# A new written order for the opening of a windowed-attention and two-MLP kernel

## The chip, the core and the metric

The kernel runs on one core of one Trainium2 chip. The metric is device time in microseconds (us) of one execution. The engines are TensorE (PE; its weight loads are listed as PEld), VectorE (DVE), ScalarE (ACT), GpSimd (POOL) and SyncE (SP), which here only issues transfers (DMA). Each engine works through its own instructions in order and waits on semaphores for the others.

## The reference

Three stages follow each other. Attention, with 4 batches, 8 heads, 512 local and 32 global tokens and a head size of 64; its result, 2176 tokens by 512, is `x`. A gated MLP with hidden size 1536, and a second MLP with hidden size 2048 and a rational function.

```python
s_g = scale * q_g @ concat(k_g, k_l).T          # global queries see all keys
out_g = softmax(s_g) @ concat(v_g, v_l)
s_ll = where(abs(i - j) <= 32, scale * q_l @ k_l.T, -1e9)
s_l = concat(scale * q_l @ k_g.T, s_ll)         # local ones see a window and the 32 globals
out_l = softmax(s_l) @ concat(v_g, v_l)
x = concat(out_g, out_l)                        # -> (2176, 512)
g = x @ w_gate                                  # 512 -> 1536
x = (g * sigmoid(g) * (x @ w_val)) @ w_out      # 1536 -> 512
h = x @ w_in                                    # 512 -> 2048
P = a0 + a1*h + a2*h**2 + a3*h**3
Q = 1 + abs(b0)*abs(h) + abs(b1)*h**2
out = (P / (Q + 1e-6)) @ moe2_w_out             # 2048 -> 512
```

The weights come as 64-bit floats.

## The kernel before, in words

**Attention** is cut into 24 units. A local unit is a block of 128 queries of one batch with all 8 heads, in two halves p of 4 heads each; a batch has 4 of them. A global unit is the 32 global queries of one batch with 4 heads; each batch has 2, and they come 4 units behind their batch's first. Units 6 and 7 are the first global ones. A unit passes through `a_score` (L247, products of queries and keys into PSUM), `a_soft` (L294: for each head a least value with the mask on DVE, L304, and an exponential with its sum on ACT, L310), `a_trans` (L335: eight PE transposes, L341, the sums' reciprocals on DVE, two copies out of PSUM, L353 or L355), `a_pv` (L362: products with the values, L374, and the division on DVE, L380) and `a_out` (L403: four PE transposes, L410, and a copy into `x32`, the token matrix, on DVE, L412).

**The first MLP** runs in two passes. Pass a, which matters here, takes the first 4 of 12 hidden blocks f (NA = 4) over 8 token chunks of 256 or 288 columns. For each chunk c and each f there are a gate product, a value product and an outward product of 12 matmuls each (`mlp`, `hidden`, `outward`). Every operand is split into a high and a low part, and each product takes three matmuls (L490 to L492). In between, `hidden` has a tanh on ACT (L518), two products on DVE (L519, L526) and the split of the result (L123 on ACT, L126 on DVE). The token chunk itself is split by `split_xy`. Outward products add up in four PSUM tiles for a chunk, and `evac_a` copies them out after its last f.

**Weights** are fetched in tiles of 512 KB (`fetch`, L131) and turned into 32-bit floats in `to_f32`: a scaling on POOL (L141), a rounding on ACT (L143), and two instructions on DVE that join the halves (L144, L146). `first_finish` then splits the first 12 tiles, which are the three tiles of each of the four f, into a high part (ACT, L123) and a low part (POOL, L126). The later 24 tiles of the first MLP are converted in the background by the loader `bg` (L634) and stored to DRAM (`w1s`, L632); it has two stage buffers and keeps one tile ahead, and a tile's fetch is issued on SP behind the store of the tile before it.

**Order.** PE and SP run in program order (`tc.manual_schedule`). The other engines' order is set by a planner. `prologue` (L583) runs units 0 and 1 (all steps), a score of unit 2, two weight tiles and the split of chunk 0. "d" words there and the table `fill` put matmuls on a tile of zeros ahead of waits, 23 of them after the first 11. Then come the pairs (c, f) in order, chunk by chunk. `inject_a` (L594) is called three times in each, ahead of the value product, ahead of the outward product and behind it; it steps the weight loaders and, by `attend` (L462), runs a part of one attention step: transposes of unit t-1; scores of unit t; values of unit t-1 and output of unit t-2. At the start of chunk 2, units 0 to 9 have their scores and units 0 to 8 their values, and 4 background tiles have been converted; 16 attention steps and 20 tiles are left for the twenty pairs of chunks 2 to 6. Chunk 7 has none.

Of the kernel before, what the change touches and what calls it, by code (L numbers as in the profile page):

```python
# [10 lines left out]
F32 = mybir.dt.float32  # L11
# [10 lines left out]
S = SL + SG  # L22
# [55 lines left out]
def tile_attn_moe_moe(  # L78
# [165 lines left out]
    st_s, st_e, st_t, st_r, st_x = {}, {}, {}, {}, {}  # L244
    ps_tag = ["a"]

    def a_score(u):  # L247
# [30 lines left out]
        a_soft(u)  # L278

    def a_score2(u):  # L280
        b, qb, ps_ = units[u]
        if qb == 4:
# [9 lines left out]
            a_soft(u)  # L292

    def a_soft(u):  # L294
        b, qb, ps_ = units[u]
        mn = att.tile([128, 8], F32, tag="mn", name="mn", bufs=3)
        sm = att.tile([128, 8], F32, tag="sm", name="sm", bufs=4)
        e = att.tile([128, 1024], F32, tag="e", name="e", bufs=2)
        if qb < 4:
            s = st_s.pop(u)  # L300
            for p in ps_:
                for hh in range(4):
                    i = 4 * p + hh
                    nc.vector.tensor_tensor_reduce(  # L304
                        out=e[:, 128 * i:128 * i + 128], in0=s[p][:, 128 * hh:128 * hh + 128], in1=msk[:, qb],
                        op0=ALU.add, op1=ALU.min, scale=-SCALE, scalar=3.0e38, accum_out=mn[:, i:i + 1],
                    )
                for i in range(4 * p, 4 * p + 4):
                    c = slice(128 * i, 128 * i + 128)
                    nc.scalar.activation(  # L310
                        e[:, c], e[:, c], AF.Exp, bias=mn[:, i:i + 1], scale=-1.0,
                        accum_out=sm[:, i:i + 1],
                    )
        else:
            s0, s1 = st_s.pop(u)
# [5 lines left out]
            )  # L321
            nc.scalar.activation(e[:, 0:384], s0[:, 0:384], AF.Exp, bias=mn[:, 2:3], scale=SCALE,
# [3 lines left out]
        st_e[u] = (e, sm)  # L326

    fill = {("t", 1): 2, ("p", 0): 2, ("p", 1): 2, ("x", 1): 3}

    def filled(o, key):  # L330
        for _ in range(fill.get(key, 0)):
            nc.tensor.matmul(o, zero[:, 0:128], zero, start=True, stop=True)
        return o

    def a_trans(u):  # L335
        b, qb, ps_ = units[u]
        e, sm = st_e.pop(u)
        t = [psum(ps_tag[0]) for p in ps_]
        filled(t[0], ("t", u))
        for i in range(4 * len(ps_)):  # L340
            nc.tensor.transpose(t[i // 4][:, 128 * (i % 4):128 * (i % 4) + 128], e[:, 128 * i:128 * i + 128], ident)  # L341
# [20 lines left out]
    def a_pv(u):  # L362
# [4 lines left out]
        if qb < 4:  # L367
# [17 lines left out]
            if n < len(local):  # L385
                load_v(local[n])
# [587 lines left out]
```

## Time and profile before

| | us |
|---|---|
| median of 3 runs | 948.02 (947.64 to 948.88) |
| span of the profiled execution | 944.1 |
| first gate product of chunk 0 starts | 22.73 |
| first gate product of chunk 2 starts | 97.12 |
| first gate product of chunk 7 starts | 247.95 |

The span reaches from the first to the last instruction of one profiled execution. A page of the profile gives the busy time of each engine, the chain of work that ended last, and groups of instructions by line. A busy PE is not a PE at its peak: matmuls are pipelined and overlap in the listing, so that the distance from one start to the next tells their cost, and an instruction that is listed as long can have waited inside. Of pass a, 8 x 4 pairs of chunk and hidden block, the first eight end at 97.12 us.

### The profile page before, as it was taken

To read this page: it belongs to the slowest core of one execution; us is meant where nothing else is said; L and a number is where in the kernel's file an instruction comes from. 1 tells how busy PE (TensorE), PEld (TensorE's weight loads), DVE (VectorE), ACT (ScalarE), POOL (GpSimd) and SP (SyncE) were. 2 spreads that over 40 slices of the span, in tenths; PEclk is the share of its full clock that TensorE was granted. 3 is DMA by queue.
4 is the path that set the end of the run, shared out by engine and by line. 5 is a ranking of instruction groups with operands and counts; after the bars stand their busy time and mean duration, and the time that the engine had idled before them with its cause. 6 is when DMAs were issued, how large, how long until landed. Compare 5 with 4: busy or idle time off the path is not lost.

```text
span 944.1 us, 20305 instructions
## 1 busy us (share of the span) xinstructions
PE 915.8 (97%) x7906; PEld 846.5 (90%) x7906; DVE 664.2 (70%) x1576; ACT 570.5 (60%) x1354; POOL 115.5 (12%) x129
## 2 busy tenths in 40 slices
PE   7789999999999999999999999999999999999997
PEld 4578878888899999999999999999999999999996
DVE  5697667766656466555432569988888888888886
ACT  5665746664344343332322368888778788788796
POOL 2440000010133244111000001000000000000032
PEclk9899999999999999999999999999999999999999
DMA  9937858853561234454522230000010010010010
GB/s 339 365 118 245 290 188 277 273 174 115 181 209 71 85 104 134 156 172 167 164 72 72 72 109 1 1 15 20 1 34 1 0 34 1 1 34 1 1 34 24
DMA packets 51169, 102.77 MB, mean 109 GB/s; under 512 B 6912, under 2 KB 25984, under 8 KB 51072
## 3 DMA queue, kind: packets, MB, share of 16 engines
q1 hardware_dynamic: 51072, 101.47, 32.5%
q8 instruction: 62, 1.02, 0.4%
q14 instruction: 35, 0.29, 0.1%
HBM read 81.01 MB, written 20.45 MB: 107 GB/s over the span
## 4 chain that ended last, share of the span: by engine, by line
PE 73%; DMA 12%; DVE 6%; ACT 3%; issue 2%; POOL 1%; SPq 1%; POOLq 0%; ACTq 0%; DVEq 0%
PE b L491 14%; PE b L490 14%; PE b L492 14%; DMA stage<-in_w_dram 10%; PE a L871 6%; PE a L872 6%; PE a L870 6%; PE a L490 4%; PE a L491 4%; PE a L492 4%; DVE stage L144 2%; DVE stage L146 2%; ACT e L310 1%; POOL stage L141 1%; DMA v<-in_vw_dram 1%
## 5 line engine op out<-in xcount | busy, mean ns | idle before, releaser
L490 PE MATMUL b<-xy,wb 128*128 128x312 f32 (+3 forms) x632 | 198.0, 313 | 0.0
L491 PE MATMUL b<-xy,wb 128*128 128x312 f32 (+3 forms) x632 | 198.0, 313 | 0.0
L492 PE MATMUL b<-xy,wb 128*128 128x312 f32 (+3 forms) x632 | 197.7, 313 | 0.0
L490 PE MATMUL b<-xy,wa 128*128 128x256 f32 (+2 forms) x400 | 125.4, 314 | 2.1 <-DVE mn L304 1.7
L491 PE MATMUL b<-xy,wa 128*128 128x256 f32 (+2 forms) x400 | 121.7, 304 | 1.2 <-DVE xy L126 1.1
L490 PEld LDWEIGHTS b<-xy,wb 128*128 128x128 f32 x632 | 118.8, 188 | 2.6
L492 PE MATMUL b<-xy,wa 128*128 128x256 f32 (+2 forms) x400 | 121.2, 303 | 0.0
L491 PEld LDWEIGHTS b<-xy,wb 128*128 128x128 f32 x632 | 118.8, 188 | 2.4
L492 PEld LDWEIGHTS b<-xy,wb 128*128 128x128 f32 x632 | 118.8, 188 | 0.0
L123 ACT CAST h<-s 128x312 fp32r<-128x312 f32 (+3 forms) x88 | 38.7, 440 | 128.7 <-DVE s L529 91.3
L820 ACT ACTIVATE t<-b,cst 128x384 f32<-128x384 f32 (+1 forms) x94 | 61.3, 652 | 56.6 <-PE b L492 53.9
L529 DVE TENSOR_TENSOR s<-s,b 128x312 f32<-128x312 f32 (+1 forms) x56 | 26.7, 476 | 94.3 <-PE b L492 89.5
L834 DVE TENSOR_TENSOR t<-t,b 128x384 f32<-128x384 f32 (+1 forms) x94 | 49.9, 531 | 44.3 <-ACT a L821 43.9
L141 POOL TENSOR_SCALAR stage<-stage 128x512 f32<-128x512 f32 x68 | 46.9, 693 | 273.7 <-DMA stage<-in_w_dram 242.7
L490 PEld LDWEIGHTS b<-xy,wa 128*128 128x128 f32 x400 | 76.3, 191 | 4.4 <-ACT e L310 1.9
L144 DVE SCALAR_TENSOR_TENSOR stage<-stage 128x512 int32<-128x512 int32 x68 | 48.6, 714 | 43.5 <-POOL stage L141 33.1
L491 PEld LDWEIGHTS b<-xy,wa 128*128 128x128 f32 x400 | 75.9, 190 | 3.3 <-DVE xy L126 2.1
L492 PEld LDWEIGHTS b<-xy,wa 128*128 128x128 f32 x400 | 75.7, 189 | 0.0
L126 DVE TENSOR_TENSOR h<-s,h 128x312 fp32r<-128x312 f32 (+3 forms) x88 | 44.1, 501 | 37.3 <-ACT h L123 37.3
L143 ACT ACTIVATE stage<-stage 128x512 int32<-128x512 uint32 x68 | 46.0, 681 | 39.2 <-DMA stage<-in_w_dram 28.0
L872 PE MATMUL a<-wb,g 128*128 128x512 f32 x170 | 66.8, 393 | 0.3 <-POOL g L844 0.3
L871 PE MATMUL a<-wb,g 128*128 128x512 f32 x170 | 67.1, 395 | 0.0
(160 smaller groups left out, 2261.8 us busy)
## 6 DMA issues: line engine op xcount, KB each, us to landing
stage<-in_w_dram SPq DMA_DIRECT2D x68, 512.0 KB, 4.3
v<-in_vw_dram SPq DMA_DIRECT2D x16, 512.0 KB, 6.6
v<-in_vw_dram SPq DMA_DIRECT2D x16, 384.0 KB, 5.5
w1s<-stage SPq DMA_DIRECT2D x24, 256.0 KB, 2.5
stage<-w1s SPq DMA_DIRECT2D x12, 512.0 KB, 6.1
w2s<-stage SPq DMA_DIRECT2D x20, 256.0 KB, 2.4
stage<-w2s SPq DMA_DIRECT2D x10, 512.0 KB, 3.7
out_dram<-x SPq DMA_DIRECT2D x17, 256.0 KB, 2.7
```

Source lines behind the costliest of these rows:

```text
L126: eng_lo.tensor_tensor(out=lo, in0=src, in1=hi.bitcast(F32), op=ALU.subtract)
L141: nc.gpsimd.tensor_scalar(out=high.bitcast(F32), in0=high.bitcast(F32), scalar1=2.0 ** -112, scalar2=1.0, op0=ALU.mult, op1=ALU.mult)
L143: nc.scalar.activation(low, low.bitcast(U32), AF.Copy, bias=0.25, scale=0.905 * 2.0 ** -29)
L144: nc.vector.scalar_tensor_tensor(out=low, in0=high, scalar=3, in1=low, op0=ALU.logical_shift_left, op1=ALU.bitwise_or)
L490: nc.tensor.matmul(o, w[:, 0, wsl], x[:, 0, xsl], start=first, stop=False)
L491: nc.tensor.matmul(o, w[:, 0, wsl], x[:, 1, xsl], start=False, stop=False)
L492: nc.tensor.matmul(o, w[:, 1, wsl], x[:, 0, xsl], start=False, stop=last)
L820: nc.scalar.activation(pt[n], h, AF.Identity, bias=NA2, scale=NA3)
L834: nc.vector.tensor_tensor(out=t, in0=t, in1=h, op=ALU.mult)
L870: nc.tensor.matmul(o, g[:, 0, gsl], w[:, 0], start=(f == 0), stop=False)
L871: nc.tensor.matmul(o, g[:, 0, gsl], w[:, 1], start=False, stop=False)
L872: nc.tensor.matmul(o, g[:, 1, gsl], w[:, 0], start=False, stop=(f == F2 - 1))
```

## The change

The first eight pairs, chunks 0 and 1, are laid out anew, with what lies before them.

- The steps of a unit become small functions (`a_least`, `a_exp`, `a_turn`, `a_copy`, `a_sums`, `a_value`, `a_norm`, `a_back`, `a_store`), as do those of a weight tile (`w_scale`, `w_round`, `w_join`, `w_high`, `w_low`), of a chunk split (`y_high`, `y_low`) and of a pair (`h_gate`, 3 of the 12 matmuls at a time, `h_tanh`, `h_times`, `h_high`, `h_low`).
- One string of words, `opening`, gives their order on every engine, also that of the transfers on SP ("@"), and for copies and low parts which of two engines has them ("*"). It covers units 0 to 7, the scores and exponentials of unit 8, the twelve first weight tiles, and chunks 0 and 1, both for f = 0, then both for f = 1, and so on. Units 0 to 3 stand ahead of the first outward product, units 0 and 1 ahead of the first gate product.
- Outward products of the two chunks share PSUM tiles, 256 columns each, which zero matmuls open; `evac_a` copies both.
- From chunk 2 on, the loop is that of before. Its twenty pairs up to chunk 7 hold 17 attention steps and 24 background tiles, two of them in each fifth pair.
- `bg` keeps three tiles ahead, over six stage buffers.
- Fillers in the opening: 3 and 5, and the first 11 stay.

The diff, cut:

```diff
+    def a_turn(u, p):
         b, qb, ps_ = units[u]
...
+        t = filled(psum(ps_tag[0]))
+        for i in range(4):
+            nc.tensor.transpose(t[:, 128 * i:128 * i + 128], e[:, 512 * p + 128 * i:512 * p + 128 * i + 128], ident)
...
-    U0 = 2
+    U0 = 9
...
+    step_at = dict(zip([n for n in range(8, 27) if n not in (12, 20)], range(U0, NU + 2)))
...
+    HALF = 256
+    seq_a = [(c, f) for f in range(NA) for c in range(2)] + [(c, f) for c in range(2, NCA) for f in range(NA)]
...
     def outward(key, f, w, first, last):
-        if first:
+        side = key == ("a", 1)
+        pair = key in (("a", 0), ("a", 1))
+        if first and not side:
             for j in range(KD):
                 accs[j] = psum("a")
+                if pair:
+                    nc.tensor.matmul(accs[j], zero[:, 0:128], zero, start=True, stop=False)
         h = hs.pop((key, f))
+        o = HALF * side
         for j in range(KD):
-            mm3(accs[j][:, :w], wt1[f, 2], slice(128 * j, 128 * j + 128), h, slice(0, w), first, last)
+            mm3(accs[j][:, o:o + w], wt1[f, 2], slice(128 * j, 128 * j + 128), h, slice(0, w),
+                first and not pair, last and (side or not pair))
...
-    prologue("s0 d4 s1 d5 t0 p0 t1 x0 p1 w x1 y s2", warm,
-             lambda: [split_xy(("a", 0), chunks_a[0], k) for k in range(KD)])
...
+    def h_gate(c, f, m, k):
+        key, w = ("a", c), HALF
+        if k == 0:
+            half[c, f, m] = filled(psum("b"))
+        mm3(half[c, f, m][:, :w], wt1[f, m], slice(128 * k, 128 * k + 128), xs[key, k], slice(0, w),
+            k == 0, k == KD - 1)
...
+    def w_round(i, eng):
+        lo = raw[i].rearrange("p (c t) -> p c t", t=2)[:, :, 0]
+        nc.scalar.activation(lo, lo.bitcast(U32), AF.Copy, bias=0.25, scale=0.905 * 2.0 ** -29)
...
+    opening = (
+        "@q0 @k0 @m0 @m1 @w0 @k1 @q1 @q2 @v00 @w1 S0 @k2 @m2 @v01 A0 F0 M00 @q3 M01 E00 @v10 S1 D0 @v11 "
+        "E01 T00 @K1 M11 C00* E11 d3 T01 R0 M10 P00 H0 C01* T11 E10 L0* @v20 F1 A1 R1 d5 T10 @q4 C11 D1 "
+        "@K0 S2 C10 @w2 H1 P01 M21 @w3 L1 S3 N0 E21 @v21 M20 P10 X0 M31 @v30 E20 P11 T21 Z0 N1 E31 @v31 "
+        "T20 R2 M30 X1 @q5 C20* Z1* T31 @w4 C21 y03* y01* C31 Y03* P20 y02* E30 y00* Y02 @v40 S4 Y01 Y00* "
+        "R3 @w5 A2 T30 F2 M40 g000 C30 v000 D2 @w6 A3 g001 v001 E40 g002 v002 M41 F3 @g g003 v003 D3 P21 "
...
+        "E6 N4 v110 v011 N5 A8 F8 @w11 X4 R6 X5 L6* Z4* T6 D8 Z5* g120 C6 g020 v111 D7 A10 g121 P6 H8 A9 "
+        "F9 g122 N6 H7 F10 v012 g021 A11 L8* g123 v013 D9 g022 v112 o00 D10 H9 i01 F11 H10 v113 L7* j01 "
+        "o10 i11 L9 v120 j11 l01 v020 D11 g023 o01 t02 u02 l11* H11 v021 L10 t12 v121 o11 u12 L11 v122 "
...
+        "u13 o02 i13 C7 S8 j03 l03 P7 M81 X6 o12 N7 E81 Z6 M80 o03 j13 E80 l13 X7 Z7 @v80 @v81 @v90 @v91 "
+    )
+    ordered = tc.manual_schedule()
+    with ordered:
+        for word in opening.split():
+            act(word)
...
-        if first.busy():
-            first.step()
-        elif c < NCA - 1 and i % 3 == 0:
-            bg.begin()
-        elif c < NCA - 1 and i % 3 == 1:
-            bg.end()
         if c < NCA - 1:
-            attend(4 * c + i // 3, i % 3)
...
+            if i == 0 or i == 1 and g % 5 == 0:
+                bg.end()
+                bg.begin()
+            else:
+                bg.end()
...
-    bg = Loader(rest_items, lambda i, x: fetch(w1[x[0], :, x[1]], const, 2), bg_back, 1)
+    bg = Loader(rest_items, lambda i, x: fetch(w1[x[0], :, x[1]], *((pro, 4) if i % 6 < 4 else (const, 2))), bg_back, 3)
```

Words of `opening`: S scores, M least values, E exponentials, T transposes, C copies, R sums, P values, N division, X output transposes, Z copy into the token matrix (of a unit and a half); F scaling, A rounding, D join, H high part, L low part (of a weight tile, three for each f); y and Y high and low part of a chunk; g and v pieces of the gate and the value product, t tanh, u and i the two products, j and l high and low part, o the outward product (of chunk and f); d fillers.

## Rows read from the trace of the kernel before

**Rows 1.** Page: busy us, share of the span and instructions by engine.
```profile
PE 915.8 (97%) x7906; PEld 846.5 (90%) x7906; DVE 664.2 (70%) x1576; ACT 570.5 (60%) x1354; POOL 115.5 (12%) x129
```

**Rows 2.** Page: chain of work that ended last, shares of the span by line.
```profile
PE b L491 14%; PE b L490 14%; PE b L492 14%; DMA stage<-in_w_dram 10%; PE a L871 6%; PE a L872 6%; PE a L870 6%; PE a L490 4%; PE a L491 4%; PE a L492 4%; DVE stage L144 2%; DVE stage L146 2%; ACT e L310 1%; POOL stage L141 1%; DMA v<-in_vw_dram 1%
```

**Rows 3.** By stretch: us, each engine's busy us, granted clock, DMA share, GB/s.
```profile
0.00:22.70 22.70, 17.96 (x377) 10.61 (x378) 12.43 (x51) 11.78 (x41) 4.58 (x11) 1.00 0.90 336
22.70:97.10 74.40, 64.48 (x1098) 54.31 (x1097) 58.51 (x196) 48.39 (x164) 24.36 (x24) 0.95 0.70 241
97.10:247.90 150.80, 144.64 (x2294) 129.89 (x2294) 100.26 (x363) 83.69 (x294) 12.51 (x19) 1.00 0.67 216
```

**Rows 4.** PE in order of time: start us, us, line, operation; two first gate matmuls.
```profile
22.73 0.47 PE L490 MATMUL b<-xy,wa 128*128 128x256 f32 x1
...
97.12 0.37 PE L490 MATMUL b<-xy,wa 128*128 128x256 f32 x1
```

**Rows 5.** PE in order of time: transposes, scores, values, and a product of twelve.
```profile
9.99 1.04 PE L341 MATMUL a<-ident,e 128*128 128x128 f32 x8
...
30.52 1.16 PE L259 MATMUL b<-k,q 64*32 64x128 f32 x64
31.61 1.10 PE L374 MATMUL b<-v,et 128*32 128x64 f32 x64
32.64 0.39 PE L490 MATMUL b<-xy,wa 128*128 128x256 f32 x1
...
34.04 0.28 PE L492 MATMUL b<-xy,wa 128*128 128x256 f32 x1
```

**Rows 6.** PE in order of time, 38 to 44 us; idle before and releaser in brackets.
```profile
38.34 3.17 PE L341 MATMUL b<-ident,e 128*128 128x128 f32 x8 [4.01 <-ACT e L310]
41.16 0.56 PE L490 MATMUL b<-xy,wa 128*128 128x256 f32 x1
...
43.65 0.41 PE L492 MATMUL b<-xy,wa 128*128 128x256 f32 x1
```

**Rows 7.** By stretch, as rows 3: two windows of 10 us.
```profile
30.00:40.00 10.00, 5.99 (x151) 4.55 (x149) 6.49 (x23) 6.04 (x19) 7.30 (x7) 0.90 1.00 380
50.00:60.00 10.00, 7.10 (x165) 5.98 (x164) 10.00 (x20) 6.18 (x15) 7.70 (x6) 1.00 0.33 112
```

**Rows 8.** Chain of work in order of time, 196 to 222 us: start, us, what.
```profile
204.51 0.69 DVE stage L144
...
206.60 4.79 DMA stage<-in_w_dram
...
212.32 0.69 DVE stage L144
```

**Rows 9.** Groups by line, 0 to 97.1 us: busy us, mean ns, idle before.
```profile
L310 ACT ACTIVATE e<-e,mn 128x128 f32<-128x128 f32 x61 | 23.6, 388 | 8.6 <-DVE mn L304 8.4
L126 POOL TENSOR_TENSOR wa<-stage,wa 128x512 fp32r<-128x512 f32 x12 | 16.7, 1406 | 21.9 <-ACT wa L123 21.9
L304 DVE CUSTOM_DVE_ANT_0 e<-b,msk 128x128 f32<-128x128 f32 x64 | 14.1, 284 | 6.1 <-PE b L259 6.1
L146 DVE SCALAR_TENSOR_TENSOR stage<-stage 128x512 int32<-128x512 int32 x16 | 12.9, 808 | 0.2
L144 DVE SCALAR_TENSOR_TENSOR stage<-stage 128x512 int32<-128x512 int32 x16 | 12.5, 781 | 5.6 <-POOL stage L141 5.3 <-issue 0.2
L123 ACT CAST wa<-stage 128x512 fp32r<-128x512 f32 x12 | 7.3, 618 | 6.6 <-DVE stage L146 6.6
L526 DVE SCALAR_TENSOR_TENSOR s<-s,b 128x256 f32<-128x256 f32 x8 | 3.3, 415 | 3.1 <-PE b L492 3.0
```

**Rows 10.** PE in order of time: the second score and what it waited for.
```profile
7.82 1.15 PE L259 MATMUL b<-k,q 64*32 64x128 f32 x64 [0.50 <-DMA k<-in_kT_dram]
```

**Rows 11.** In order of time, 18 to 24 us: POOL's subtraction and DVE's join.
```profile
19.23 1.27 POOL L126 TENSOR_TENSOR wa<-stage,wa 128x512 fp32r<-128x512 f32 x1 [1.04 <-ACT wa L123]
20.01 1.07 DVE L146 SCALAR_TENSOR_TENSOR stage<-stage 128x512 int32<-128x512 int32 x1
```

More of the change, by code (lines that the diff above doesn't have):

```diff
@@ L321, in a_soft, with a_exp @@
             )
+    def a_exp(u, p):
+        b, qb, ps_ = units[u]
+        e, sm, mn = st_e[u]
+        if qb < 4:
+            for i in range(4 * p, 4 * p + 4):
+                c = slice(128 * i, 128 * i + 128)
+                nc.scalar.activation(
+                    e[:, c], e[:, c], AF.Exp, bias=mn[:, i:i + 1], scale=-1.0,
+                    accum_out=sm[:, i:i + 1],
+                )
+        else:
+            s0, s1 = st_s[u]
             nc.scalar.activation(e[:, 0:384], s0[:, 0:384], AF.Exp, bias=mn[:, 2:3], scale=SCALE,
@@ L360, in a_trans, with copy_on, a_copy @@
-        st_t[u] = (et, rc)
-    def a_pv(u):
+    def copy_on(eng, out, in_):
+        (eng.copy if eng is nc.scalar else eng.tensor_copy)(out, in_)
+    def a_copy(u, p, eng):
+        if u not in st_et:
+            st_et[u] = att.tile([128, 1024], F32, tag="et", name="et", bufs=2)
+        t = st_t.pop((u, p))
+        copy_on(eng, st_et[u][:, 512 * p:512 * p + 512], t[0])
+        if units[u][1] == 4:
+            copy_on(eng, st_et[u][:32, 512:640], t[1][:32, 0:128])
+    def a_trans(u):
+        ps_ = units[u][2] if units[u][1] < 4 else (0,)
+        for p in ps_:
+            a_turn(u, p)
+        a_sums(u)
+        for p in ps_:
+            a_copy(u, p, nc.scalar)
@@ L397, in a_pv, with a_norm @@
                     )
+    def a_norm(u):
+        b, qb, ps_ = units[u]
+        rc, o = st_r.pop(u), st_o.pop(u)
+        x = st_x[u] = att.tile([128, 8, 64], F32, tag="x", name="x", bufs=2)
+        if qb < 4:
+            nc.vector.tensor_tensor(
+                out=x, in0=o.rearrange("p (h d) -> p h d", h=8),
+                in1=rc.unsqueeze(2).to_broadcast([128, 8, 64]), op=ALU.mult,
+            )
+        else:
             for j in range(2):
@@ L464, in attend @@
             t = step_at[n]
-            for fn, u in (((a_trans, t - 1),), ((a_score, t), (a_score2, t)), ((a_pv, t - 1), (a_out, t - 2)))[part]:
-                run(fn, u)
+            for fn, u in (((a_trans, t - 1),), ((a_scores, t),), ((a_pv, t - 1), (a_out, t - 2)))[part]:
+                if U0 <= u < NU or u == U0 - 1 and fn is not a_scores:
+                    begun.add((fn, u))
+                    fn(u)
     xs, hs, accs = {}, {}, {}
@@ L610, in inject_a @@
         state["n"] += 1
-        if c == NCA - 1 and i % 2 == 1:
+        if c == NCA - 1 and (3 * g + i) % 2:
             rest.begin()
@@ L681, in tile_attn_moe_moe @@
             rest.prefetch(4)
[L682 to L692 removed]
+        hidden(("a", c), f, w, inject_a)
+        out_a()
+        inject_a()
+        prev = (c, f, w)
+        if c == NCA - 1:
+            split_xy(("b", 0), chunks_b[0], f)
     def evac_b(c):
```

376 lines of the change are left out of this document (224 added, 152 removed), and 6 rows, old and new, of the table opening.

## The prediction

> **What bounds the kernel now.** I read four views in this order. First the busy times of the page: TensorE (PE) is busy 97% of the span, VectorE (DVE) 70%, ScalarE (ACT) 60% [rows 1]. The reader should distrust that 97%: the same page's chain of work that ended last gives 10% of the span to waits for incoming weights, `stage<-in_w_dram` [rows 2], and a PE that never stops would not be waited for by anything. So the next views are a table by stretch [rows 3], the matmuls in order of time, and the chain itself. Call a pair of token chunk and hidden block f a slot. PE starts the first gate product of chunk 0 at 22.7 us, and that of chunk 2 (slot 8) at 97.12 us [rows 4]; the change rewrites what lies before that point. From 22.7 to 97.1 us there are eight slots in 74.4 us: PE busy 64.5, DVE 58.5, PE's mean granted clock 0.95. From 97.1 to 247.9 us (slots 8 to 27) there are twenty slots in 150.8 us, PE busy 144.6 [rows 3].
>
> The busy 64.5 us is not 64.5 us of work. Eight slots need 8 x 36 matmuls less the 12 of the last outward product, 276; twelve run from 32.64 to 34.04 and one more step, 0.116 each [rows 5], which makes 32.0 us. The attention pieces in that stretch (7 scores at 1.09; transposes 1.04 and values 1.03 for 5 local units; 0.65 each for 2 units of global queries, that is 5/8 of a local one, an estimate; 4 output transposes at half of 1.04 [rows 5]) make 22.8. A first matmul after a change of kind shows 0.39 against 0.28 [rows 5]; some 28 changes make 3. That is 58 of 74.4 us: 78%. The other 16 us are waits, some hidden inside "busy" (eight transposes show 3.17 us instead of 1.04), and one spell at half clock: after 4.01 idle us twelve matmuls run from 41.16 to 43.65, 0.21 each [rows 6]. What is waited for: DMA is still saturated from 30 to 40 us (380 GB/s) and lies nearly idle from 50 us on (112 GB/s), where DVE is full, 10.00 of 10 [rows 7]. Twelve weight tiles come late, and each must be rounded, joined and split before a slot can run.
>
> In the middle stretch something else holds: later weights are converted one tile per slot, in a closed ring. The chain shows it: join on DVE at 204.51, the next fetch issued behind the store, 4.79 us of DMA from 206.60, GpSimd's (POOL) scaling, join again at 212.32 [rows 8]. That is 7.8 us a turn; the slots take 150.8 / 20 = 7.54.
>
> **The change, part by part.** *What stays:* every product, transfer and conversion. From slot 28 (247.9 us) on the program is the same, so I take the 696.2 us of the span that follow as unchanged, and so the 3.9 us between the span of 944.1 and the median of 948.0.
>
> *The opening.* Units 0 to 3 come ahead of the first gate product, chunks 0 and 1 share each weight tile, and all engines follow one written list. I summed the list's words per engine up to its end, where slot 8 begins. Prices: exponentials 0.388 each, four to a piece; join 0.808 + 0.781; high part of a weight 0.618 on ACT, low part 1.41 on POOL; the half-chunk steps (tanh, both products, high and low parts) 0.41; least values 0.22 each (14.1 us for 64) [rows 9]; PE's pieces as above. Per engine:
> to the first gate product: PE 14.4, DVE 18.3, ACT 18.0;
> then to outward product (0,1): PE 31.4, DVE 35.1, ACT 28.5, POOL 14.4;
> then to the end: PE 17.0, DVE 10.6, ACT 9.0, POOL 6.3.
> Totals: PE 63 (64 gate and value pieces of 3 matmuls, 7 outward products, 9 scores, 6 local and 2 global units behind them, 8 fillers in place of 23), DVE 64, ACT 55.5.
>
> First stretch. ACT has the rounding of weight 0 written ahead of its first exponential, so it waits for the fifth transfer of the queue. Before, the fifth (keys) was there when the second score started, at 7.82 after waiting for it [rows 10]; I take 8.3, and 8.3 + 18.0 = 26.3 us for the first gate product, against 22.7. DMA doesn't forbid that: what the list fetches up to weight 2 is 8.3 MB, and before, 336 GB/s over 22.7 us [rows 3] moved 7.6. Bounds: 24 if weight 0 is there at once, 28 if each unit repeats the score's latency.
> Second stretch. DVE is longest, 35.1; PE with its changes needs 33. In its fullest slice DVE was busy 10.00 of 10 [rows 7]; I take 94%, 37.3, so 63.6 us. Bounds: 35.1 (no wait) and 42 (PE at its old 78%).
> Third stretch. PE 17.0, changes 1.3, waits 0.5: 18.8, so slot 8 starts at 82.4. Bounds: 17 and 23.5 (78%).
> Sum: 82.4 - 97.1 = **-14.7**; the bounds are 24 + 35.1 + 17 = 76 (-21) and 26.3 + 42 + 23.5 = 92 (-5). What covers the parts costed at nothing: the dropped fillers lay in waits; ACT's 55.5 us lie beside DVE's 64. SP's queue waits in written order for value and stage buffers, and the transfers behind such a wait are wanted 10 us later or more: nothing, or one landing of 4.79 us [rows 8] if that cover is gone.
>
> Joins beside POOL's subtraction stretch: one took 1.07 us beside a 1.27 us subtraction [rows 11], against 0.69 for the join at 204.51 [rows 8]; the crowded mean is 0.808 and 0.781 [rows 9]. I priced the pair at that mean, 1.59. The Trainium skill, "GPSIMD Engine Reference", section "Key points", says that GpSimd shares its SBUF interfaces with VectorE and contends with instructions that have two SBUF inputs, which speaks against a list that keeps both full at once. By that rule at its strongest, each half of a join at 1.07, the ten joins of the second stretch would cost 10 x (2.14 - 1.59) = 5.5 us more.
>
> *The middle.* Added: one local unit's scores, transposes and values move from before slot 8 to behind it (17 steps of attention instead of 16): 1.09 + 1.04 + 1.03 and changes, 3.5 on PE, which is the path there. Four more conversions (24 tiles in 20 slots instead of 20): 4 x 1.4 on DVE, which is busy 100 of 150.8 us [rows 3], nothing. Twice the copies from the first accumulators: 0.4. Removed: the ring. The loader keeps three tiles ahead over six buffers, so the 4.79 us of DMA leave it. What is late next is PE itself: of 150.8 us it idles 6.2 [rows 3], and no more can come back. I take half, 3.1 (the other half I put down to exponentials and copies of the same slot). Sum: 3.5 + 0.4 - 3.1 = **+0.8**; bounds -2.3 (all comes back) and +3.9 (none does).
>
> Total: 948.0 - 14.7 + 0.8 = **934** us; bounds 925 and 947.
>
> **The rivals.**
> A. The opening stays as loose as it was: PE at 78% from the first gate product on, slot 8 at 92, total 944. Joins at 1.07 go part of the way, 940. For it: engines still wait in order, and a late piece holds all behind it. Against: the chief cause, weight tiles that come one by one for a single chunk, meets twice the work per tile.
> B. It closes up: second and third stretch without waits and all 6.2 us back, 925 to 928. For it: DVE did run 10 us without a gap. Against: PE, DVE and ACT within a few us of each other rarely all fit.
> C. It doesn't do what it says: tiles are as late as before, since DMA is saturated up to 40 us either way, and two chunks wait together: slot 8 at 96 to 98, total 947 to 950. Against: nine of the twelve tiles are wanted only after some 30 us.
> D. Slower, by the clock: 8 fillers stand in place of 23, and PE has 45.8 us of work in its first 64. If its pauses reach the 4 us after which the clock stood at half before [rows 6], a matmul costs 0.21 instead of 0.116, and the second stretch takes twice 33 us instead of 37.3: 963. It decides once the half clock covers some 18 us of work there (4 us of PE's slack and the 13.9 us of gain). Against: its pieces lie 1 to 2 us apart, and with PE busy 18.0 of the first 22.7 us the clock was 1.00 [rows 3].
>
> **How the numbers follow.** Forecast (929 to 940) 0.58; A 0.20; B 0.11; C 0.05; D 0.06. The range takes in the forecast, B but its edge, and A: 926 to 945. A measurement of this kernel can tell 0.2% (1.9 us) from no change. Faster: forecast, A, B and a little of C, 0.90; same: most of C, 0.04; slower: D, 0.06.
>
> **What would show it.** After the change: first gate product at 26 us (24 to 28), outward product (0,1) done near 64, first gate product of chunk 2 near 82, PE's clock 1.00 throughout, DVE over 90% busy from 26 to 64 us. Slots 8 to 27 in 150 to 153 us, with the DMA of weights gone from the chain there. I am wrong if the first gate product comes after 30 us, if the clock falls, or if the middle takes under 147 or over 156 us.

## The result and the profile after

The changed kernel takes 937.52 us (median of 4 runs, 935.89 to 941.21); the kernel before, beside it, 948.45 (947.64 to 948.91). The ratio is 0.9901, with a 95% interval of 0.9871 to 0.9930. On another chip, unedited, it took 936.99 (934.29 to 938.81) beside 945.71 (940.83 to 948.07), ratio 0.9917 (0.9891 to 0.9944). The forecast was 934, range 926 to 945.

The milestones of the profiled executions, in us (the first profile after is that of the fastest of its four runs, 935.89):

| | before | forecast | after | after, a second execution |
|---|---|---|---|---|
| first gate product of chunk 0 | 22.73 | 26.3 | 32.06 | 32.45 |
| outward product (0,1) done | | 63.6 | 69.63 | 70.07 |
| slot 8 starts | 97.12 | 82.4 | 87.65 | 88.02 |
| slot 28 starts | 247.95 | 234.0 | 243.33 | 243.07 |
| pass b starts | 270.82 | 256.9 | 264.26 | 263.04 |
| span | 944.1 | 930.1 | 934.1 | 936.1 |

So against the kernel before the opening gained 9.5 us (forecast 14.7), slots 8 to 27 lost 4.8 (forecast 0.8), chunk 7 gained 1.9 and the rest 3.4 (forecast 0 for both): 9.9 in all.

First the page's busy times, which answer to [rows 1]; then the stretches of [rows 3], cut at the changed kernel's own marks (us, each engine's busy us, granted clock, DMA share, GB/s):

```profile
PE 908.7 (97%) x7893; PEld 845.8 (91%) x7895; DVE 664.0 (71%) x1578; ACT 569.4 (61%) x1348; POOL 116.9 (13%) x133
```
```profile
0.00:32.06 32.06, 22.74 (x538) 15.69 (x540) 18.19 (x90) 18.93 (x75) 5.08 (x12) 0.89 0.95 342
32.06:69.63 37.57, 33.92 (x546) 30.56 (x548) 34.18 (x92) 26.98 (x77) 16.83 (x18) 0.95 0.64 236
69.63:87.65 18.02, 17.59 (x245) 16.19 (x243) 9.73 (x41) 7.36 (x29) 4.87 (x6) 1.00 0.44 160
87.65:243.33 155.68, 149.64 (x2432) 134.40 (x2430) 112.46 (x396) 93.66 (x320) 17.84 (x26) 0.99 0.73 243
```

The second and third stretch came out as summed: 37.6 and 18.0 us, forecast 37.3 and 18.8. The first, with PE busy for only 22.7 of 32.1 us at a clock of 0.89, and the last didn't.

PE in order of time, for the first stretch and slot 8 (start, us, line; in brackets the idle time before and what ended it; answers to [rows 4] and [rows 10]):

```profile
10.54 1.73 PE L259 MATMUL b<-k,q 64*32 64x128 f32 x64 [4.04 <-DMA q<-in_qT_dram]
...
19.23 1.09 PE L259 MATMUL b<-k,q 64*32 64x128 f32 x57
23.67 0.42 PE L259 MATMUL b<-k,q 64*32 64x128 f32 x7 [3.35 <-issue]
...
32.06 0.36 PE L526 MATMUL b<-xy,wa 128*128 128x256 f32 x1
...
87.65 0.36 PE L526 MATMUL b<-xy,wa 128*128 128x256 f32 x1
```

Two things are new against [rows 10]. The second score waited 4.04 us for its queries, to 10.54 instead of 7.82, since weight 0 stands ahead of them in the queue. And in the middle of one score, 57 of its 64 matmuls done, PE stood still for 3.35 us, and the releaser is "issue": nothing that the profile shows was waited for.

ScalarE in order of time shows where the 5.8 us of the first stretch went:

```profile
8.78 0.66 ACT L669 ACTIVATE stage<-stage 128x512 int32<-128x512 uint32 x1 [6.77 <-DMA stage<-in_w_dram]
9.34 0.39 ACT L325 ACTIVATE e<-e,mn 128x128 f32<-128x128 f32 x1
...
24.54 0.40 ACT L325 ACTIVATE e<-e,mn 128x128 f32<-128x128 f32 x1 [2.19 <-DVE mn L306]
...
28.84 0.59 ACT L374 COPY x<-a 128x512 f32<-128x512 f32 x1 [2.65 <-PE a L448]
```

The rounding of weight 0 started at 8.78 instead of the assumed 8.3: 0.5 us. Behind it ACT's work was to run without a gap; it stood idle for 2.19 us (least values of the score in which PE had stood) and for 2.65 us (PE, late by then and at half clock), and 0.7 in two short waits. Together that is 6.0 us. ACT's own work from 8.78 on was 17.6 us, 0.4 less than the 18.0 of the sum, and what is left is the lateness, 5.8. PE's mean clock there was 0.85:

```profile
8.78:32.06 23.28, 17.65 (x463) 13.45 (x465) 16.13 (x72) 17.64 (x74) 4.38 (x6) 0.85 1.03 389
```

### The profile page after: what moved, and what is told of

Read it like the earlier page. It is cut to its first block, busy times and chain, and to the rows that moved or that the text cites. A ratio compares the mean times of both kernels' runs of the same rounds, so it can differ in the third digit from the quotient of the medians.

```text
span 934.1 us, 20234 instructions
## 1 busy us (share of the span) xinstructions
PE 908.7 (97%) x7893; PEld 845.8 (91%) x7895; DVE 664.0 (71%) x1578; ACT 569.4 (61%) x1348; POOL 116.9 (13%) x133
## 4 chain that ended last, share of the span: by engine, by line
PE 84%; DMA 6%; DVE 4%; ACT 2%; issue 2%; SPq 1%; POOL 0%; POOLq 0%; ACTq 0%; DVEq 0%
PE b L526 15%; PE b L528 15%; PE b L527 15%; PE a L1056 7%; PE a L1055 6%; PE a L1054 6%; PE a L526 5%; PE a L527 4%; PE a L528 4%; DMA stage<-in_w_dram 4%; PE b L259 1%; PE b L354 1%; PE b L404 1%; DMA q<-in_qT_dram 1%; PE a L354 1%
## 5 line engine op out<-in xcount | busy, mean ns | idle before, releaser
L123 ACT CAST h<-s 128x312 fp32r<-128x312 f32 (+3 forms) x80 | 35.5, 444 | 118.2 <-DVE s L565 91.7
L1018 DVE TENSOR_TENSOR t<-t,b 128x384 f32<-128x384 f32 (+1 forms) x94 | 49.9, 531 | 41.5 <-ACT a L1005 41.3
L141 POOL TENSOR_SCALAR stage<-stage 128x512 f32<-128x512 f32 x56 | 39.2, 700 | 226.0 <-DMA stage<-in_w_dram 174.9
L1056 PE MATMUL a<-wb,g 128*128 128x512 f32 x170 | 67.1, 395 | 0.3 <-POOL g L1028 0.3
L1006 ACT ACTIVATE q<-a,cst 128x384 f32<-128x384 f32 (+1 forms) x94 | 64.9, 691 | 3.0
L1054 PE MATMUL a<-wb,g 128*128 128x512 f32 x170 | 66.3, 390 | 0.5 <-ACT g L1041 0.5
L1055 PE MATMUL a<-wb,g 128*128 128x512 f32 x170 | 66.7, 392 | 0.0
L126 DVE TENSOR_TENSOR h<-s,h 128x312 fp32r<-128x312 f32 (+3 forms) x80 | 39.4, 493 | 35.0 <-ACT h L123 34.8
```

The source lines that it names most:

```text
L123: nc.scalar.copy(hi, src)
L126: eng_lo.tensor_tensor(out=lo, in0=src, in1=hi.bitcast(F32), op=ALU.subtract)
L141: nc.gpsimd.tensor_scalar(out=high.bitcast(F32), in0=high.bitcast(F32), scalar1=2.0 ** -112, scalar2=1.0, op0=ALU.mult, op1=ALU.mult)
L1006: nc.scalar.activation(pq[n], a, AF.Identity, bias=B0, scale=B1)
L1018: nc.vector.tensor_tensor(out=t, in0=t, in1=h, op=ALU.mult)
L1054: nc.tensor.matmul(o, g[:, 0, gsl], w[:, 0], start=(f == 0), stop=False)
```

## The experiments

Each kernel was run beside the kernel before on its chip. The chips and executions differ, so where a few us are at stake I compare milestones as well as medians. Eight profiles have the changed kernel's order on PE from slot 8 on, with its whole conversion and loader (the two of the table and those of six experiments: fillers, small matmuls, keys first, the two with VectorE's load, the spare tile): their slots 8 to 27 take 152.7 to 159.1 us, 155.8 in the mean. The six that leave the opening wholly unedited but for a memset (the two of the table, old loader, no conversion, later joins, spare tile) start slot 8 at 85.7 to 88.5. A milestone inside these spreads shows nothing.

**Small matmuls and fillers ahead of the second score.** Two edits of the changed kernel, each a word in the written order. `B` is a score more, 64 matmuls into a tile that nobody reads; `W16` is 16 fillers.

```diff
-@q3 M01 E00 @v10 S1 D0 @v11
+@q3 M01 E00 @v10 B S1 D0 @v11
```

```diff
-@q3 M01 E00 @v10 S1 D0 @v11
+@q3 M01 E00 @v10 W16 S1 D0 @v11
```

> The changed kernel with 32 score products of 64 matmul records and 64 weight loads more (128 PE instructions, about 1.15 us of PE) between the first and the second score, written to an unused PSUM tile, where PE idles from 6.5 to 10.5 us anyway. Theory K: PE's instructions arrive in blocks of 256, the next block is asked for when PE enters the one before, and while DMA is full that takes about 5.8 us (PE stood still without a wait at record 705 and 1473, 768 apart). Then half a block more costs about 2.9 us: first gate product at 35 us instead of 32.1, the whole by 2 to 3 us slower. Rival R: those stops are chance and the first stretch is late only because the second score's keys and queries lie behind weight 0: nothing changes, within 0.5 us.

> The changed kernel with 16 full filler matmuls (32 PE instructions, 3.4 us of PE) in the same place. Theory K: an eighth of a block, 0.7 us later, against which the clock stays whole at 10.9 to 14.3 us, worth up to 1 us: together within 0.5 us. Rival C: the half clock is what made the first stretch late: first gate product 1.5 to 2 us earlier, the whole as much faster.

The small matmuls gave 938.91 us (936.71 to 946.04), ratio 0.9938 (0.9904 to 0.9972), first gate product 34.85, slot 8 at 87.36. The fillers gave 939.74 (935.52 to 943.75), ratio 0.9945 (0.9922 to 0.9969), 32.33 and 87.77. They kept the second score at full clock (1.15 us instead of 1.73) and the first gate product came no sooner, so half clock at that score isn't what made it late. Where PE stood in the kernel with small matmuls, in order of time; then, by stretch up to a stop, the matmuls and weight loads that PE had behind it (counts in brackets), first for that kernel up to its stops at 21.46 and 27.49 (a third, at 34.65, lies just ahead of its first gate product), then for the changed kernel and the one with fillers:

```profile
21.46 0.44 PE L404 MATMUL a<-v,et 128*32 128x64 f32 x7 [3.46 <-issue]
27.49 0.42 PE L404 MATMUL a<-v,et 128*32 128x64 f32 x12 [0.86 <-issue]
...
34.65 0.44 PE L354 MATMUL a<-ident,e 128*128 128x128 f32 x2 [2.10 <-issue]
```
```profile
0.00:21.40 21.40, 15.20 (x348) 9.57 (x348) 9.89 (x53) 12.45 (x47) 3.34 (x9) 0.97 0.93 325
0.00:27.40 27.40, 20.37 (x475) 13.45 (x476) 13.04 (x71) 15.64 (x63) 3.34 (x9) 0.88 0.95 342
```
```profile
0.00:22.50 22.50, 14.65 (x347) 9.35 (x348) 11.58 (x62) 14.05 (x55) 3.28 (x9) 0.92 0.93 328
```
```profile
0.00:23.00 23.00, 17.36 (x348) 9.81 (x348) 11.31 (x62) 13.85 (x55) 3.32 (x9) 0.96 0.93 330
```

The stop moved from a score (L259) to a product with the values (L404), another piece of work, but not in the count: 695 or 696 matmuls and loads each time. With the ten waits that are instructions of their own the trace has 705 or 706 records on PE ahead of it, and in the kernel with small matmuls 961, 255 or 256 further on, ahead of the next. The changed kernel's other stop is at 1473, three times 256 behind the first. The stop is no wait of the program; it belongs to a place in PE's instruction stream. That instructions are fetched there can be seen: between 20.5 and 23.5 us the table of transfers has one packet of 0.02 MB in the instruction queue beside a data queue that is full:

```profile
q1 hardware_dynamic: 682, 1.15, 102.3%
q8 instruction: 1, 0.02, 2.0%
```

That packet lands at 22.3 and PE goes on at 23.67. The queue has 62 such packets of 16 KB for PE's 15 895 records (7893 matmuls, 7895 weight loads, the rest waits), one for each 256. In the fourteen profiles PE pauses 40 times for over 0.3 us without a wait; each of these pauses has 192 to 194 records ahead of it beyond a multiple of 256, and each ends 1.2 to 1.6 us behind the end of such a packet. So the stops are waits for instructions. They aren't confined to the opening: the changed kernel's second profile has one at record 6849, and the one with fillers four in slots 8 to 27, 5.2 us in all, which is more than its 159.1 us there lie above the mean.

```profile
211.86 0.29 PE L528 MATMUL b<-xy,wa 128*128 128x288 f32 x1 [1.45 <-issue]
```

What the data queue has to do with it wasn't tried with fewer bytes. And the count of 64 matmuls made the first gate product 2.8 us later but not slot 8: lateness of that milestone is taken up behind it.

**Keys and queries ahead of weight 0.** The scaling, the rounding and VectorE's join of weight 0 move behind the second score as well.

```diff
-@q0 @k0 @m0 @m1 @w0 @k1 @q1 @q2 @v00 @w1 S0 @k2 @m2 @v01 A0 F0 M00 @q3 M01 E00 @v10 S1 D0
+@q0 @k0 @m0 @m1 @k1 @q1 @w0 @q2 @v00 @w1 S0 @k2 @m2 @v01 M00 @q3 M01 E00 @v10 S1 A0 F0
-E01 T00 @K1 M11 C00*
+E01 T00 @K1 M11 D0 C00*
```

> The changed kernel with the second score's keys and queries ahead of weight 0 in the transfer queue, and weight 0's scaling, rounding and join behind the first exponentials and least values. Theory K together with the place of weight 0: second score at 8 us instead of 10.5, so that PE enters its blocks 2.5 us earlier; first gate product at 29.5, slot 8 at 85, the whole 2 to 3 us faster. Rival W: the wait moves with weight 0 to the join and the first split, and the first gate product stays at 32 us, the whole within 0.7 us.

Measured: 934.05 us (933.31 to 934.99), ratio 0.9881 (0.9834 to 0.9928), the lowest ratio of all complete kernels. But the first gate product moved by 0.4 us only (31.71), though the second score started 2.0 us sooner: PE stood still in the same place of its stream, for 3.32 us, and went on at 21.97 instead of 23.67.

```profile
8.57 1.15 PE L259 MATMUL b<-k,q 64*32 64x128 f32 x64 [2.14 <-DMA q<-in_qT_dram]
...
21.97 0.65 PE L259 MATMUL b<-k,q 64*32 64x128 f32 x7 [3.32 <-issue]
```

Slot 8 is at 85.65, which the unedited opening with the spare tile reached as well (85.67), and the interval overlaps that of the changed kernel. So the late queries alone are not what made the first stretch long (weight 0's conversion moved back with the edit, and its share isn't told apart), and the gain isn't shown.

**VectorE lighter, VectorE heavier.** My sum took VectorE as the longest engine of the second stretch. Seven of its pieces go to GpSimd and ScalarE (4.2 us); in the other kernel it has five subtractions (`K`, 128x512, into a tile that nobody reads) more.

```diff
-A4 i00 X3 C41* S5 j00 F4
+A4 i00 X3 C41 S5 j00 F4
...
-F6 v101 y13* A6 g102 L2* v102 E51
+F6 v101 y13 A6 g102 L2 v102 E51
```

```diff
-Y13 @w8 g013 D4 @w9
+Y13 @w8 g013 D4 K @w9
...
-C50 S6 D6 @w10
+C50 S6 D6 K @w10
```

> The changed kernel with seven pieces taken off VectorE in the second stretch of the opening, 4.2 us of its time by the profile's durations: four low parts go to GpSimd, a scores' copy and two evacuations of y go to ScalarE. Theory (VectorE's sum of work sets the second stretch, as the prediction took it, 35.1 of 37.3 us): slot 8 moves from 87.65 to 84 to 86. Rival one (order and hand-overs set it): slot 8 stays within 0.7 us. Rival two: GpSimd's four low parts come late and hold gate products back, slot 8 is later by 1 to 3 us. The middle isn't touched.

> The changed kernel with five subtractions of 128x512 more on VectorE (into a tile that nobody reads), spread over the second and third stretch of the opening, some 3.3 us of its time. Theory (VectorE's sum of work sets the stretch): slot 8 moves from 87.65 to 90.2 to 91.2. Rival (order and hand-overs, or TensorE, set it): slot 8 moves by less than 1 us, since the added work falls into VectorE's waits. The middle isn't touched.

Lighter: 933.69 us (932.92 to 937.19), ratio 0.9893 (0.9866 to 0.9921), slot 8 at 88.46; its profile is that of the slowest of its four runs. Heavier: 940.15 (936.92 to 942.38), ratio 0.9957 (0.9934 to 0.9980), slot 8 at 92.30. The second stretch of both, then the third kernel to put beside them, one with an unedited opening in which the clock didn't fall there (the spare tile, below):

```profile
32.40:70.51 38.11, 34.27 (x547) 30.64 (x548) 33.55 (x84) 27.16 (x78) 22.76 (x22) 0.96 0.63 231
```
```profile
31.55:74.29 42.74, 36.08 (x550) 32.31 (x548) 38.76 (x96) 25.87 (x76) 16.14 (x18) 0.88 0.56 209
```
```profile
31.46:67.65 36.19, 32.58 (x548) 29.17 (x548) 33.63 (x92) 27.05 (x77) 16.77 (x18) 1.00 0.67 246
```

Lighter didn't come out lighter: VectorE's busy time hardly fell, 33.6 us against 34.2, while GpSimd's rose from 16.8 to 22.8. The groups by line of that stretch say why (busy us, mean ns, idle before):

```profile
L676 DVE SCALAR_TENSOR_TENSOR stage<-stage 128x512 int32<-128x512 int32 x10 | 9.9, 993 | 0.3
L674 DVE SCALAR_TENSOR_TENSOR stage<-stage 128x512 int32<-128x512 int32 x10 | 8.6, 857 | 0.0
L641 DVE TENSOR_TENSOR xy<-x,xy 128x256 fp32r<-128x256 f32 x4 | 3.6, 929 | 0.0
```

A join's halves take 0.857 and 0.993 us, in the changed kernel 0.763 and 0.789 (below); the subtractions of chunk splits 0.929 against 0.654. That is 10 x 0.298 + 4 x 0.275 = 4.1 us, as much as the edit took away. What VectorE gave to GpSimd it paid back beside it, and so this kernel doesn't tell whether VectorE sets the stretch; whether its three faster runs differ there wasn't profiled.

Heavier does, in part. The five subtractions took 0.770 each, 3.85 in all, and the stretch 5.2 us more (42.74 against 37.57). The clock explains most of that: at a mean of 0.88 over 42.7 us it lost 5.1 us, at 0.95 the changed kernel's lost 1.7 of 37.6. Without that it is 37.6 against 35.9, so by this estimate, from one profile each, 1.7 us of the 3.85 were on the path and the rest went into VectorE's waits. Both my theory and the rival are half right: VectorE has some 2 us to spare before all that is added to it lengthens the stretch, and longer pauses of PE (idle 6.7 us there, 3.7 in the changed kernel) came with a fallen clock.

From the first gate product to slot 8 the picture is simple. PE was busy 50.0 us at full clock (small matmuls, keys first, spare tile: 49.9, 50.0, 50.2) and 51.5 to 51.8 where the clock fell to a mean of 0.97, with some 4 us idle (2.6 with small matmuls); that is 92% of the stretch, and in the third one 98%. PE's own work is most of what is left there.

**The loader, both ways.** The kernel before with the new loader, and the changed kernel with the old one.

```diff
-    bg = Loader(rest_items, lambda i, x: fetch(w1[x[0], :, x[1]], const, 2), bg_back, 1)
+    bg = Loader(rest_items, lambda i, x: fetch(w1[x[0], :, x[1]], *((pro, 4) if i % 6 < 4 else (const, 2))), bg_back, 3)
```

> The kernel before with the changed kernel's background loader alone (three tiles ahead, six staging buffers, the opening as before). Theory: the ring of load, conversion and release holds the middle of the kernel before to 7.8 us a tile, and going three deep gives back up to the 6.2 us that TensorE stands idle there; the last conversions are then read earlier, as in the changed kernel, which was worth 1.9 us in chunk 7. Expected: slots 8 to 27 take 144.5 to 150.8, with 147.7 as the middle of it, chunk 7 begins 3 to 8 us earlier, the total 3 to 8 us shorter, ratio 0.992 to 0.997. Rival: the exponentials, not the ring, set the middle of the kernel before; then slots 8 to 27 stay within 1 us of 150.8 and the total within 1 us (ratio 0.999 to 1.001).

> The changed kernel with the old background loader (one tile ahead, two stage buffers) and all else as changed. Theory ring (that of the prediction): a turn of 7.8 us for each of 24 tiles, 187 us for slots 8 to 27 instead of 155.7; the whole 25 to 31 us slower. Rival P: the ring had slack and PE sets the pace; slots 8 to 27 within 3 us of 155.7, and the two tiles of each fifth slot are caught up in slots without attention.

The new loader alone: 941.23 us (938.01 to 945.48), ratio 0.9976 (0.9956 to 0.9995). The old loader in the changed kernel: 960.68 (959.03 to 964.01), ratio 1.0164 (1.0119 to 1.0209). Slots 8 to 27 and chunk 7 of the first, slots 8 to 27 of the second:

```profile
97.21:247.12 149.91, 143.64 (x2292) 129.61 (x2293) 104.31 (x372) 87.71 (x305) 14.89 (x20) 1.00 0.65 223
...
247.12:266.88 19.76, 19.66 (x147) 19.29 (x145) 13.46 (x24) 8.38 (x20) 5.25 (x4) 1.00 0.55 179
```
```profile
86.54:254.77 168.23, 154.73 (x2432) 136.88 (x2430) 109.59 (x394) 91.54 (x317) 13.82 (x21) 0.97 0.63 203
```

In the kernel before, the ring wasn't the bound of the middle: 149.9 against 150.8 us [rows 3], and PE idles 6.3 us (0.9 of it a stop for instructions), before 6.2. The new loader's gain lies in chunk 7, 19.8 us against 22.9, where the kernel before still finished the last conversions: its last join ended at 251.0 us, inside chunk 7, that of the changed kernel at 234.7. With 24 tiles to carry in 20 slots the ring does become the bound: 168.2 us are 7.0 a tile, and VectorE waits 27.3 us there for GpSimd's scaling, 11.0 in the changed kernel. The new loader earns 12.5 us of slots 8 to 27 in the changed kernel and hardly anything in the middle of the kernel before. The other half of the old loader's 23 us lies behind slot 28: from the start of pass b on its profile takes 681.3 us, those of the changed kernel 669.9 and 673.1. Its first 120 gate and value matmuls there take 29.8 us instead of 25.6, with PE waiting and at half clock; most of the rest is a slower pace of PE.

**No conversion in the middle.** ScalarE copies the high words of a background tile and nothing else is done: the kernel leaves out the conversion, and the second pass multiplies by these words as they stand.

```diff
+    def high_words(fetched):
+        st = fetched[0]
+        nc.scalar.copy(st[:, 0:512].bitcast(F32), st.rearrange("p (c t) -> p c t", t=2)[:, :, 1].bitcast(F32))
+        return st[:, 0:512].bitcast(F32)
...
-    bg = Loader(..., bg_back, 3)
+    bg = Loader(..., bg_back, 3, front_fn=high_words)
```

> The changed kernel, in which the splitting of the background tiles of the gate weight during slots 8 to 27 is left out: ScalarE copies the high words once, and VectorE's join and GpSimd's low parts are gone, so that the second pass gets weights without their low halves. Theory: the middle lost its 4.9 us to the extra unit and to joins that wait in VectorE's order for GpSimd and for late stages; without them slots 8 to 27 fall from 155.7 to 148 to 152. Rival: TensorE's own work and the exponentials set it, and it stays at 154 to 156; ScalarE then even has one copy more. The opening up to slot 8 isn't touched: 87.0 to 88.3.

Measured: 930.13 us (928.99 to 931.91), ratio 0.9850 (0.9827 to 0.9874), and for slots 8 to 27:

```profile
86.67:238.11 151.44, 147.91 (x2431) 132.53 (x2430) 84.07 (x349) 93.64 (x321) 1.77 (x2) 1.00 0.75 251
```

151.4 us is below all eight of the other profiles (mean 155.8, least 152.7), and 2.0 of the 3.5 us that PE idles there are stops for instructions: by this one profile the conversion costs some 4 us, although VectorE is busy for 112 of 155.7 us only. The longest of PE's waits shows one way in which it does; the chain of work of the changed kernel near 200 us (start, us, what; answers to [rows 8]):

```profile
181.93 8.48 DMA stage<-in_w_dram
...
192.36 0.26 SPq L808
...
193.17 4.96 DMA stage<-in_w_dram
...
198.29 0.66 POOL stage L141
...
198.99 0.69 DVE stage L144
199.68 0.20 DVE e L306
...
200.67 0.37 PE b L526
```

The fetch is issued at 193.2 only, behind a store of `y` (L808) that SP's queue had to let go first; the join stands in VectorE's order ahead of the least values of a score (L306), and PE waits 2.06 us. The transfers of weights that the new loader was to take off the path are on it here. They have 22% of the chain in slots 8 to 27 (35% in the second profile), in the kernel before 43%: less, but not gone as forecast.

**Joins one slot later.** GpSimd's scaling and ScalarE's rounding of a tile are issued a slot ahead of the joins and the store, in the changed kernel and in the one with keys first.

```diff
...
+    def bg_back(i, item, ready):
+        st, low, high = ready
+        nc.vector.scalar_tensor_tensor(out=low, in0=high, scalar=3, in1=low,
...
+        nc.vector.scalar_tensor_tensor(out=st[:, 0:512], in0=high, scalar=-2 ** 31, in1=low,
...
                 bg.end()
                 bg.begin()
-            else:
-                bg.end()
```

> The changed kernel with one edit in the middle: GpSimd's scaling and ScalarE's rounding of a background tile are issued one slot before VectorE's two joins and the store, instead of all in one. No work is left out. Theory (the 4.2 us that leaving the conversion out gave back in slots 8 to 27 were VectorE standing in front of joins, 11.0 us of waits for GpSimd's scaling): slots 8 to 27 fall from 155.7 to 152 to 154, the total by 1.5 to 4. Rival (it was the joins' own work and their transfers): within 1 us of 155.7. Opening and second MLP as in the changed kernel.

> The later joins together with the opening in which keys and queries of unit 0 come ahead of weight 0 (which alone gave slot 8 at 85.65 and 934.05). By the theory that the two gains lie in different stretches and add up: slot 8 at 85 to 86.5, slots 8 to 27 in 152 to 154, total 930 to 933. Rival: the later joins give nothing, or half of the earlier gain was the two spells of half clock that stayed away by chance; then 933.5 to 938.

Both theories fell: 942.94 us (937.95 to 945.88), ratio 0.9973 (0.9950 to 0.9996), and 941.60 (937.93 to 944.15), ratio 0.9960 (0.9942 to 0.9978). Slots 8 to 27 took 164.6 us (profiled in the slowest of twelve runs) and 161.5, and most of the loss is in slots 8 to 11, 41.8 us against 34.7 and 40.6 against 35.4 with keys first alone. The chain there, in the changed kernel with later joins, and PE in order of time:

```profile
97.35 1.15 SPq L829
98.56 5.14 DMA stage<-in_w_dram
103.72 0.59 ACT stage L819
104.35 0.37 ACT y L804
104.72 0.83 ACT e L325 x5
...
105.69 2.11 ACT e L325 x11
107.80 0.26 ACT y L804
108.11 0.58 PE a L526
```
```profile
108.11 0.58 PE L526 MATMUL a<-h,wa 128*128 128x256 f32 x1 [4.81 <-ACT y L804]
108.49 0.42 PE L527 MATMUL a<-h,wa 128*128 128x256 f32 x1
```

The store moved a slot back, and with it the fetch behind it on SP (L829, then the transfer at 98.56). The rounding now waits for that transfer in ScalarE's order, and behind it stand 16 instructions of exponentials and the copies of the accumulators that PE needs: 4.81 us idle, and then matmuls 0.21 us apart instead of 0.116. The wait wasn't removed; it went to an engine on which more depended. VectorE's waits for GpSimd's scaling in slots 8 to 27 are 13.2 us, 11.0 before the edit.

**The changed kernel again, and a spare tile.** The second has a tile of 2 KB a partition more, and one memset.

```diff
+    spare = att.tile([128, 512], F32, name="spare")
+    nc.vector.memset(spare[:, 0:8], 0.0)
```

> The changed kernel once more, unedited, for a second profile of it and as the measure of the kernels beside it. Expected by the theory that the marks of one program agree between executions within 1 us except for spells of half clock: first gate product 31.5 to 32.7, slot 8 at 86 to 88.5, slots 8 to 27 in 154.5 to 156.5, total 935 to 940. The second MLP's pace was 8.293 us a pair in the changed kernel and 8.373 before: if that belongs to the program, 8.293 comes again; if it belongs to the execution, either may come.

> The changed kernel with an unused tile of 2 KB a partition in the attention's pool and one memset of 8 columns on VectorE at the start, as in the kernel with five extra subtractions but without these. That kernel ran the second MLP at 8.373 us a pair instead of 8.293. If where the tiles lie in memory sets the pace, 8.373 comes here too and the total rises by 3 us; if it is the execution or the order of instructions, 8.293 and 935 to 940. The opening isn't touched beyond the memset: slot 8 at 86 to 88.5. For the theory that TensorE's own work sets the second and third stretch: 50 us of busy time between the first gate product and slot 8 plus 1.7 for each spell of half clock of 3.4 us, plus 4 us idle, here again within 1 us.

Again: 936.99 us (934.29 to 938.81). Spare tile: 935.66 (931.44 to 939.66), ratio 0.9910 (0.9877 to 0.9944). Here are 100 us of the second MLP, the changed kernel's first profile and the second one:

```profile
660.00:760.00 100.00, 100.00 (x508) 90.99 (x507) 87.04 (x176) 80.12 (x153) 0.00 (x0) 1.00 0.03 9
```
```profile
660.00:760.00 100.00, 100.00 (x504) 90.96 (x503) 86.04 (x174) 79.33 (x152) 0.00 (x0) 1.00 0.03 9
```

The same program did 508 matmuls in one execution and 504 in the other, at the same granted clock; the kernel before did 503. A pair takes 8.293 or 8.373 us, 3 us over this MLP. So 3.2 of the 3.4 us that the rest had gained in the first profile belong to the execution and not to the change. The two executions were on different chips, but two of the three chips used for the experiments showed both paces, one of them 8.293 with VectorE lighter and 8.373 with VectorE heavier. That the tiles' place in memory sets the pace isn't borne out: the spare tile ran at 8.373, but so did the unedited kernel. What sets it stays open.

## Why the prediction was right, and where it wasn't

The total was right to 3.5 us of a gain forecast at 14.0, and it fell into the forecast's own case, not into rival A or B. The 3.9 us between span and median, taken as unchanged, came out as 3.4. By its steps:

- *First gate product at 26.3, bounds 24 to 28: wrong, 32.06, past the point at which I said I would be wrong.* The mechanism, ACT's 18.0 us of work behind weight 0's rounding, was right (17.6 us from 8.78 on). The step that failed is that this work runs without a gap. It idled 5.5 us, 4.8 of it behind PE's stop of 3.35 us inside a score and the half clock that went with it; no run was without that stop, so how much of it is the stop's and how much the clock's stays open. A stop that no wait shows couldn't be read from the rows that I took; the kernel before has one too, of 1.1 us.
- *Second stretch 37.3, third 18.8: 37.6 and 18.0.* The price list held. The reason given for the second, VectorE as the longest engine, held in part: what was added to it cost 1.7 us of 3.85, plus the clock. It and PE, 34.2 and 33.9 of 37.6 us busy, share the bound, and no run parts them further. Of the 37.6 us, 1.7 are half clock that I had put at none.
- *Joins beside GpSimd at 1.59 the pair.* Ten pairs came out at 0.763 + 0.789 = 1.55. Which of the 20 halves pay shows when they are taken one by one: 14 met no GpSimd instruction and took 0.69 us, two lay beside one for four fifths of their time or more and took 1.33. In the kernel with VectorE lighter it was 9 at 0.69 and 8 at 1.12, and the pair took 1.85. The rule of the Trainium skill, "GPSIMD Engine Reference", section "Key points", that GpSimd contends with VectorE's instructions that have two SBUF inputs, agrees with that; at its strongest (2.14 the pair) it wasn't met, as few halves met GpSimd.

```profile
L676 DVE SCALAR_TENSOR_TENSOR stage<-stage 128x512 int32<-128x512 int32 x10 | 7.9, 789 | 0.3
L674 DVE SCALAR_TENSOR_TENSOR stage<-stage 128x512 int32<-128x512 int32 x10 | 7.6, 763 | 0.0
```

- *Opening -14.7, bounds -21 to -5: -9.5.* Slot 8 lies at 85.7 to 88.5 in six executions of the unedited opening, so -8.6 to -11.4. All of the miss is the first stretch.
- *Middle +0.8, bounds -2.3 to +3.9: +4.8, just outside, 4.2 in the second profile.* The added unit and copies, 3.9, were priced well: PE is busy 5.0 us more in the first profile (1.7 of it half clock) and 3.5 more in the second (33.4 + 114.7 against 144.6). The term that failed is the 3.1 us that were to come back from the ring: PE idles 6.0 us, as before (6.2). I had read the ring's 7.8 us a turn beside 7.54 us a slot as the bound; the new loader alone shows that it wasn't. The upper bound left out half clock (1.7 us in the first profile) and stops for instructions (1.45 in the second).
- *From slot 28 on unchanged: wrong by 1.9 us in the good direction.* Conversions that reached into chunk 7 end sooner, and the new loader alone brings that too (3.1).
- *The clock stays at 1.00: wrong.* It was 0.89 and 0.95 in the first two stretches. Rival D's mechanism acted, at less than a fifth of its price of 29 us: by the means, 3.5 us in the first stretch, part of it beside waits, and 1.7 in the second.

The forecast's two misses, 5.2 in the opening and 4.1 in the middle, were made good by 1.9 in chunk 7 and by 3.4 behind it. Nearly all of the 3.4 was luck: the second execution's span is 936.1.

## What to carry to other kernels

A chain that passes through a stage's transfers isn't proof that they set the pace: ask how much the engine behind them idles, and compare two profiles of one program before a few us in an untouched stretch are put down to a change. When a conversion is split or handed on, look at what stands behind each of its instructions in each engine's order and at the fetch that its store releases on the transfer queue; here the wait went from VectorE to ScalarE and cost 7 us. Work that a full engine gives to GpSimd must be priced on both: what VectorE gave, it paid back in longer instructions. Where an engine stands still and no wait ends it, count its instructions up to the stop in two kernels.

## What the hardware showed

- PE stood still without any wait at fixed counts of its instruction stream, multiples of 256 apart (449 or 450, 705 or 706, 961, 1218, 1472 or 1473 and later ones up to 6850), for 0.4 to 4.4 us: 3.35 us in the changed kernel, 4.39 in its second profile, 3.46 with the count reached by other work. PE went on 1.2 to 1.6 us behind the end of a 16 KB packet of the instruction queue each time. In the first 45 us the data queue was full beside them; behind that not always, as with 1.17 us at 95.3 without conversion, where DMA was 43% busy in the 4 us up to it. The Trainium skill, "Runtime: NRT & Kernel Launch", section "Instruction fetch mechanics", says that instructions come in blocks of 256 and that crossing from one to the next is mostly hidden. The distance agrees, and so does "mostly" by count: the changed kernel's first profile shows two stops of over 0.3 us in 62 blocks. But these two were not hidden, and most of the opening's miss lies behind one of them. A score alone, 64 matmuls and 64 loads, runs through half such a distance in 1.1 us; whether sparser pieces avoid the stop wasn't tried.
- VectorE's instructions with two operands in SBUF got longer where a GpSimd instruction ran beside them: half a join 0.69 us without, 1.33 and 1.12 beside one. Least values, with an operand in PSUM, kept theirs (0.283 and 0.282 in the same two kernels). GpSimd's busy share alone doesn't tell it: the pair took 1.55 us at 45% and 1.85 at 60%, but 1.68 at 38% with VectorE heavier.
- PE's granted clock fell to half in spells at different times in executions of one program: in slots 8 to 27 the changed kernel's first profile had 0.99, its second 1.00. In the second stretch both had 0.95, the spare tile's, with the same order, 1.00.
- The second MLP, with PE without a pause and the clock at 1.00, ran at two paces, 8.293 and 8.373 us a pair, in two executions of one program, and the same two in the experiments (a third, 8.427, with the old loader).
